# First two batches in three runs over the hidden columns, with the weight conversions spread over 36 units

## The chip, the core and the metric

The kernel runs on one core of a Trainium2 chip. The metric is the device time of one execution in microseconds; of two kernels the one with the lower time is better. A core has five engines that run side by side, each with an in-order queue of its own: PE multiplies matrices into PSUM, DVE and POOL do elementwise work, ACT does activations and copies, and SP issues the DMA transfers. POOL cannot read PSUM.

## The reference

For 8 batches of 8 heads, attention runs twice (32 packed queries `p` attend to `k` and `v`, then `q` attends to the packed result), and two feed-forward layers follow:

```
p_packed = softmax(p @ k.T * scale) @ v
x = softmax(q @ p_packed.T * scale) @ p_packed      # 4608 tokens x 512 after the heads are joined
h = x @ w_in                                        # 512 -> 2048
x = (max(h, 0) + alpha * min(h, 0)) @ w_out         # 2048 -> 512
out = (silu(x @ w_gate) * (x @ w_val)) @ w_out2     # 512 -> 1536 -> 512
```

The inputs of attention are 32-bit floats. The weight matrices are 64-bit floats, and the kernel converts them on the chip.

## The kernel before, in words

**Stage 1** makes attention and the first layer, **stage 2** (`gv_step`) the second layer. Stage 1 is a list `order` of 256 units. A unit is one half batch `j` (288 tokens) and one of 16 groups `f` of 128 hidden columns. `h_unit` makes six matmuls with the attention weights `a2` and the product `ppw` of the packed result with `w_in`. ACT then scales the result (`m`, L1003), DVE makes the activation `g` (L1006), ACT rounds it to `hi` (L1014), and POOL subtracts to get `lo` (L1016). Three units later `o_unit` adds twelve matmuls with `w_out` into four PSUM banks `acc`. At the end of a half batch's run over `f` the four banks are emptied: to DRAM as a partial sum `x1p` if columns are still to come, and with the earlier partial sum added (L1047) otherwise. A run that follows cannot start in the banks until they are empty.

**Order of the units.** Batches 0 and 1 (half batches 0 to 3) share their weights: first f = 0..7 for all four, then f = 8..15 for all four, 64 units in all. The other batches follow one by one.

**Conversion of a weight piece.** `w_in` and `w_out` come as 16 pieces each, `i0`..`i15` and `o0`..`o15`, one per f; an entry `1` in a script calls `convert()` for the next piece of `ORDER`. `widen` loads a piece, takes its high words with ACT (L222), and forms the float on DVE (L224, L228, L237, L246, and L254 for three pieces in four); POOL adds the parts (L265, and L252 in place of L254 for eight pieces). A piece of `w_out` costs two more steps on ACT (L283, L284) and one on POOL (L285). The tiles are called `cva` and `cvb`.

**Attention of batches 0 and 1** is done by `quad` for four groups of heads: a and b are batch 0, c and d batch 1. The scripts name its steps: `c.kt0` turns keys with PE and copies them out of PSUM with ACT (L338), `c.s1`, `c.et`, `c.pp`, `c.ppt` make the packed result, `c.s2` and `c.a2` the second softmax (DVE L497 to L534; for d two of its steps are on POOL). `w01` makes `ppw` of batch 0 for f = 4..7 (PE L795, ACT L799, DVE L800).

**What sets the order of the work around the units** is written by hand. `START` runs ahead of unit 0. `EARLY` has a key (unit, 0 or 1): the script runs ahead of or behind `h_unit` of that unit. `BEHIND` puts loads of c and d behind the load of a certain weight piece in SP's queue. `HOLD` delays four of ACT's L222 steps. From unit `CHAIN0` on, PE takes its work in the order in which it is written; ahead of it a scheduler may order PE's work otherwise. Slots from `GROUP0` on are also given to the conversion of stage 2's weights.

Of the kernel before, what the change touches and what calls it, by code (L numbers as in the profile page):

```python
# [17 lines left out]
P = 128  # L18
# [7 lines left out]
LOADS = "b.v a.v 1", "a.q 1 1 b.q"  # L26
START = """
    a.kt0 b.kt0 a.pt a.kt1 b.kt1 b.pt a.s1 a.et a.pp b.s1 a.ppt b.et b.qt0 a.qt0 b.pp b.qt1 a.qt1
    a.s20 b.ppt b.s20 a.a20 b.a20 1 1 1 1 1 w00 1 1
"""  # L30
EARLY = {
    (0, 0): "c.pd d.pd",
    (0, 1): "c.pt 1 b.s21 c.kt0 c.kt1",
    (1, 0): "c.s1",
    (1, 1): "d.kt0 d.pt 1 c.et d.qt0 c.pp",
    (2, 0): "c.qt0",
    (3, 0): "w01 d.qt1 a.s21",
    (3, 1): "c.ppt b.a21",
    (4, 1): "1 d.kt1 d.s1 a.a21 c.qt1",
    (5, 1): "1",  # L40
    (6, 1): "1 d.et",
    (7, 0): "d.pp",
    (7, 1): "1",
    (10, 1): "c.s2 d.ppt d.s2 w10",
    (11, 1): "1",
    (13, 0): "d.a2",
    (15, 0): "c.a2",
    (17, 1): "w11",
    (18, 1): "1 1",
    (20, 1): "1 1",  # L50
    (21, 1): "1",
    (23, 1): "1",
    (24, 1): "1",
    (25, 1): "1 1",
    (26, 1): "1 1",
    (27, 1): "1 w02",
    (28, 1): "w03",
    (33, 1): "1",
    (36, 1): "w12 w13",
    (37, 1): "1 1",  # L60
}

ORDER = """
    i2 o2 i0 i3 i1 o0 o3 o1 i5 i4 i7 i6 o5 o4 o7 o6
    i13 i10 i11 o13 i15 i8 i14 i9 i12 o10 o14 o8 o9 o12 o11 o15
"""

BEHIND = {"c.k": 3, "c.q": 4, "c.v": 5, "d.k": 5, "d.q": 6, "d.v": 9}

BY_POOL = {0, 2, 4, 7, 11, 18, 23, 29}  # L70
HOLD = {15: 5, 16: 7, 17: 15, 19: 16}


STEPS = """
# [8 lines left out]

LEAVE = (6, 7, 38, 39)

CHAIN0 = 36

# [15 lines left out]
def f32(ap):  # L105
    return ap.bitcast(F32)
# [3 lines left out]
def tile_kernel(  # L110
# [23 lines left out]
    nc = tc.nc  # L134
    B, H, S, D = q.shape
# [79 lines left out]
    def widen(src, raw, val, out=None, n_piece=-1):  # L215

        issued.append(nc.sync.dma_start(out=like(raw, src), in_=src))
        words = raw.rearrange("p (n t) -> p n t", t=2)
        low, high = words[:, :, 0], words[:, :, 1]
        held = n_piece in HOLD  # L220
        with tc.issue_after(begun[HOLD[n_piece]].ins) if held else ExitStack():
            nc.scalar.activation(out=f32(val), in_=f32(high), func=AF.Abs)  # L222
        yield "v"
        nc.vector.tensor_scalar(  # L224
            out=f32(val), in0=f32(val), scalar1=E_TOP, scalar2=E_LOW, op0=ALU.min, op1=ALU.max
        )
# [639 lines left out]
    def at(it, late, fn):  # L866

        plan.setdefault((it, late), []).append(fn)

    order = []
    for bs in [(0, 1)] + [(b,) for b in range(2, B)]:
        for fs in (range(NF1 // 2), range(NF1 // 2, NF1)) if len(bs) > 1 else (range(NF1),):
            for j in range(2 * bs[0], 2 * bs[-1] + 2):
                order += [(j, f, f == fs[0], f == fs[-1]) for f in fs]

    NB1 = 2 * NF1
    busy = set()
# [98 lines left out]
    def load_part(j):  # L978
        part[j] = [utile("x", [P, 2, HS], f"x1p{j}_{pr}") for pr in range(2)]
        for pr in range(2):  # L980
            nc.sync.dma_start(out=part[j][pr], in_=x1p[j][:, 2 * pr : 2 * pr + 2, :])
# [37 lines left out]
    def o_unit(it):  # L1019
# [17 lines left out]
        if not stop:  # L1037
            return
        if f != NF1 - 1:
            x1p[j] = dram.tile([P, KC, HS], F32, name=f"x1p{j}")  # L1040
        dst = x1d[j] if f == NF1 - 1 else x1p[j]
        for pr in range(2):
            xs = part[j][pr] if j in part else utile("x", [P, 2, HS], f"x1s{it}_{pr}")
# [7 lines left out]
                    nc.scalar.activation(out=xs[:, i, :], in_=a, func=AF.Copy)  # L1051
            nc.sync.dma_start(out=dst[:, 2 * pr : 2 * pr + 2, :], in_=xs)

    for j in range(4):
        at(NB1 + 8 * j + 6, 0, lambda j=j: load_part(j))


    raw2, xs2, gvw, wo2, ps2, acc2, outs = {}, {}, {}, {}, {}, {}, {}
# [303 lines left out]
```

## Time and profile before

| what | us |
|---|---|
| time of three executions, median | 1705.68 |
| lowest, highest of them | 1702.39, 1712.24 |
| span of the profiled execution, first to last instruction | 1709.4 |

The profiled execution's time outside its span is not on its page, so the span stands for it: it is 3.7 us over the median and inside the three times. The page divides the span into busy time of engines, and the trace behind it gives every instruction with its start, its duration and what it waited for. Times in the rows are microseconds from the span's start unless marked ns. A busy time counts the time that an instruction takes on its engine, waits inside it included.

### The profile page before, as it was taken

Reading aid. Unit: us, or ns where it says so; the run is one execution under the profiler, and the core shown is the slowest. Engines: PE = TensorE matmul, PEld = TensorE weight load, DVE = VectorE, ACT = ScalarE, POOL = GpSimd, SP = SyncE. Lnnn points to the kernel's source line nnn. Section 1 sums busy time; section 2 is a strip of 40 time slices with the busy share of each in tenths; the row PEclk is TensorE's granted clock in tenths of the full one; section 3 lists DMA queues with packets and bytes.
Section 4 is the critical chain, followed back from the end, with each engine's and each line's share of the span. In section 5 each row is a group of like instructions: output and inputs, shape, how many; then the busy total and the mean of one; then the engine's idle time right before and its main releaser. Section 6 shows DMA issues by size and latency. Waiting matters only on the chain.

```text
span 1709.4 us, 28545 instructions
## 1 busy us (share of the span) xinstructions
PE 1614.0 (94%) x10708; PEld 1458.3 (85%) x10708; DVE 923.8 (54%) x1621; ACT 683.4 (40%) x1511; POOL 804.6 (47%) x824
## 2 busy tenths in 40 slices
PE   5698999999998989999999999999999999999997
PEld 3467798988888878889899999999999999999997
DVE  5989757555656646565533543553453454354332
ACT  5774645545544545555522231232232232123222
POOL 3656744655554654547633443443443443343343
PEclk8899999999999999999999999999999999999999
DMA  9433464635445452644573463455455456445442
GB/s 232 123 103 111 121 161 115 163 95 149 133 117 133 119 139 63 150 128 151 181 275 141 174 235 140 164 198 185 165 209 178 162 184 201 163 173 176 163 173 80
DMA packets 227370, 266.11 MB, mean 156 GB/s; under 512 B 130464, under 2 KB 189856, under 8 KB 227232
## 3 DMA queue, kind: packets, MB, share of 16 engines
q1 hardware_dynamic: 227232, 264.30, 48.8%
q8 instruction: 84, 1.38, 0.3%
q14 instruction: 54, 0.44, 0.1%
HBM read 214.70 MB, written 49.55 MB: 155 GB/s over the span
## 4 chain that ended last, share of the span: by engine, by line
PE 70%; DVE 8%; DMA 6%; POOL 5%; issue 5%; ACT 4%; SPq 2%; DVEq 0%; POOLq 0%; ACTq 0%
PE o L306 6%; PE o L307 6%; PE o L305 6%; PE acc L1029 5%; PE yb L305 4%; PE acc L1035 4%; PE acc L1030 4%; PE yb L307 4%; PE yb L306 4%; PE vb L306 3%; PE vb L307 3%; PE vb L305 3%; PE xb L306 3%; PE xb L307 3%; PE xb L305 3%
## 5 line engine op out<-in xcount | busy, mean ns | idle before, releaser
L1016 POOL TENSOR_TENSOR lo<-g,hi 128x288 fp32r<-128x288 f32 x256 | 226.2, 885 | 244.0 <-ACT hi L1014 188.8
L1223 POOL TENSOR_TENSOR s<-s,p 128x384 f32<-128x384 f32 x72 | 73.2, 1016 | 468.7 <-ACT s L1222 468.7
L1006 DVE SCALAR_TENSOR_TENSOR g<-h,sg,m 128x288 f32<-128x288 f32 x256 | 130.4, 510 | 163.5 <-ACT m L1003 129.0
L305 PE MATMUL h<-a2h,ppw 128*128 128x288 f32 x512 | 163.0, 318 | 27.5 <-DVE g L1006 21.5
L1184 DVE TENSOR_TENSOR u<-vb,u 128x384 f32<-128x384 f32 x144 | 80.3, 558 | 190.5 <-PE vb L307 189.6
L1014 ACT ACTIVATE hi<-g 128x288 fp32r<-128x288 f32 x256 | 113.0, 442 | 155.2 <-DVE g L1006 151.3
L307 PE MATMUL o<-wp,ph 128*128 128x512 f32 x432 | 171.4, 397 | 0.0
L306 PE MATMUL o<-wp,ph 128*128 128x512 f32 x432 | 170.9, 396 | 0.0
L305 PE MATMUL o<-wp,pl 128*128 128x512 f32 x432 | 168.7, 391 | 1.0 <-POOL pl L1249 1.0
L1249 POOL TENSOR_TENSOR pl<-s,ph 128x384 fp32r<-128x384 f32 x144 | 145.4, 1031 | 32.3 <-ACT ph L1247 32.3
L1222 ACT ACTIVATE s<-p 128x384 f32<-128x384 f32 x72 | 37.9, 526 | 301.8 <-DVE p L1184 301.8
L307 PE MATMUL h<-a2l,ppw 128*128 128x288 f32 x512 | 153.3, 300 | 0.0
L306 PE MATMUL h<-a2h,ppw 128*128 128x288 f32 x512 | 153.1, 299 | 0.0
L305 PEld LDWEIGHTS h<-a2h,ppw 128*128 128x128 f32 x512 | 98.4, 192 | 62.3 <-DVE g L1006 30.7
L305 PE MATMUL yb<-ring,gv 128*128 128x384 f32 x432 | 146.0, 338 | 3.6 <-DVE u L1184 3.4
L306 PE MATMUL yb<-ring,gv 128*128 128x384 f32 x432 | 144.4, 334 | 0.0
L307 PE MATMUL yb<-ring,gv 128*128 128x384 f32 x432 | 144.4, 334 | 0.0
L1003 ACT ACTIVATE m<-h,sal 128x288 f32<-128x288 f32 x256 | 125.6, 492 | 44.0 <-PE h L307 43.0
L1184 DVE TENSOR_TENSOR u<-yb,p 128x384 f32<-128x384 f32 x144 | 79.4, 551 | 116.9 <-PE yb L307 107.0
L1247 ACT ACTIVATE ph<-s 128x384 fp32r<-128x384 f32 x144 | 74.7, 525 | 148.3 <-DVE s L1227 133.3
L1229 POOL TENSOR_TENSOR s<-s,u 128x384 f32<-128x384 f32 x72 | 98.9, 1373 | 5.6
L1210 DVE TENSOR_TENSOR s<-xb,s 128x384 f32<-128x384 f32 x72 | 40.1, 557 | 110.0 <-ACT s L1209 110.0
(234 smaller groups left out, 4409.6 us busy)
## 6 DMA issues: line engine op xcount, KB each, us to landing
gv<-wgvd SPq DMA_DIRECT2D x144, 896.0 KB, 6.2
wgvd<-cva SPq DMA_DIRECT2D x84, 256.0 KB, 2.5
cva<-in_moe_w_out_dram SPq DMA_DIRECT2D x28, 512.0 KB, 3.7
v<-in_v_dram SPq DMA_DIRECT2D x16, 576.0 KB, 5.5
out_dram<-os SPq DMA_DIRECT2D x12, 768.0 KB, 3.8
cva<-in_moe_w_in_dram SPq DMA_DIRECT2D x16, 512.0 KB, 4.1
kr<-in_k_dram SPq DMA_DIRECT2D x96, 72.0 KB, 2.7
qr<-in_q_dram SPq DMA_DIRECT2D x96, 72.0 KB, 2.5
```

The lines of the kernel that those rows point to most:

```text
L305: nc.tensor.matmul(o, wlo, xhi, start=start, stop=False, **kw)
L306: nc.tensor.matmul(o, whi, xhi, start=False, stop=False, **kw)
L307: return nc.tensor.matmul(o, whi, xlo, start=False, stop=stop, **kw)
L1003: begun[it] = nc.scalar.activation(out=m, in_=hp, func=AF.Copy, scale=sal[:, f : f + 1])
L1006: made[it] = nc.vector.scalar_tensor_tensor(out=g32, in0=hp, scalar=sg[:, f : f + 1], in1=m, op0=ALU.mult, op1=ALU.max)
L1014: rounded[n] = nc.scalar.activation(out=hi, in_=x, func=AF.Copy)
L1016: nc.gpsimd.tensor_tensor(out=lo, in0=x, in1=f32(hi), op=ALU.subtract)
L1029: nc.tensor.matmul(acc[dc], lo[:, f % WP, c], ghi, start=start, stop=False)
L1184: return nc.vector.tensor_tensor(out=out, in0=bank, in1=x, op=ALU.add)
L1229: nc.gpsimd.tensor_tensor(out=s2, in0=s2, in1=u3, op=ALU.mult)
L1247: nc.scalar.activation(out=hi, in_=x, func=AF.Copy)
L1249: nc.gpsimd.tensor_tensor(out=lo, in0=x, in1=f32(hi), op=ALU.subtract)
```

## The change

The list `order` now goes through the first two batches in three runs over f: columns 0..3 for the four half batches (units 0 to 15), columns 4..7 (units 16 to 31), and columns 8..15 (units 32 to 63, as before). Each half batch therefore stores two partial sums and loads two, where it stored one and loaded one. `ORDER`, `EARLY`, `START`, `BEHIND`, `HOLD` and `CHAIN0` follow:

```
-    a.s20 b.ppt b.s20 a.a20 b.a20 1 1 1 1 1 w00 1 1
+    a.s20 b.ppt b.s20 a.a20 b.a20 1 1 1 1 1 w00
 EARLY = {
-    (0, 1): "c.pt 1 b.s21 c.kt0 c.kt1",
...
-    (10, 1): "c.s2 d.ppt d.s2 w10",
...
-    (36, 1): "w12 w13",
-    (37, 1): "1 1",
+    (0, 1): "c.pt c.kt0 c.kt1",
...
+    (6, 0): "d.a2",
+    (6, 1): "w10",
     (7, 1): "1",
...
+    (36, 1): "1",
+    (44, 1): "w12",
+    (48, 1): "w13",
...
-BEHIND = {"c.k": 3, "c.q": 4, "c.v": 5, "d.k": 5, "d.q": 6, "d.v": 9}
+BEHIND = {"c.k": 3, "c.q": 4, "c.v": 5, "d.k": 5, "d.q": 6, "d.v": 7}
...
-HOLD = {15: 5, 16: 7, 17: 15, 19: 16}
+FIRST_RUNS = (4, 4, 8)
...
-CHAIN0 = 36
+CHAIN0 = 4
...
-        held = n_piece in HOLD
-        with tc.issue_after(begun[HOLD[n_piece]].ins) if held else ExitStack():
-            nc.scalar.activation(out=f32(val), in_=f32(high), func=AF.Abs)
+        nc.scalar.activation(out=f32(val), in_=f32(high), func=AF.Abs)
...
+    for n in FIRST_RUNS:
+        for j in range(4):
+            if f0:
+                again.append((len(order) + n - 1, j))
+            order += [(j, f, f == f0, f == f0 + n - 1) for f in range(f0, f0 + n)]
+        f0 += n
+    for j in range(4, NHALF):
+        order += [(j, f, f == 0, f == NF1 - 1) for f in range(NF1)]
...
-            x1p[j] = dram.tile([P, KC, HS], F32, name=f"x1p{j}")
+            x1p[j] = dram.tile([P, KC, HS], F32, name=f"x1p{j}_{f}")
...
-    for j in range(4):
-        at(NB1 + 8 * j + 6, 0, lambda j=j: load_part(j))
+    for it, j in again:
+        at(it, 1, lambda j=j: load_part(j))
```

Eight pieces are now converted in `START` (ten before), none in units 0 to 6, and the other 24 from unit 7 to unit 36, mostly one a unit. Up to unit 39 both kernels convert all 32.

DVE's queue between the activations `g32_2` and `g32_3` of units 2 and 3, before (`cva` and `cvb` are tiles of a weight piece):

```order
L1006 SCALAR_TENSOR_TENSOR g32_2_732<-h2_725,sg_98,m_2_733 128x288
L246 TENSOR_SCALAR cva1_102<-cva1_102 128x512
L224 TENSOR_SCALAR cvb0_103<-cvb0_103 128x512
L228 TENSOR_SCALAR cvb0_103<-cvb0_103 128x512
L237 SCALAR_TENSOR_TENSOR cvb0_103<-cva0_101,cvb0_103 128x512
L1006 SCALAR_TENSOR_TENSOR g32_3_778<-h3_771,sg_98,m_3_779 128x288
```

The same place in the change (lines have moved by 11 or 16; `s2t_0`, `a_0` are group a's second softmax, `mx_3`, `sums_3` group d's first):

```order
L528 TENSOR_REDUCE sx_0_373<-s2t_0_372 128x9
L529 TENSOR_SCALAR sx_0_373<-sx_0_373 128x9
L530 RECIPROCAL sx_0_373<-sx_0_373 128x9
L427 TENSOR_REDUCE mx_3_703<-s11_3_700 128x1
L531 TENSOR_TENSOR s2t_0_372<-s2t_0_372,sx_0_373 128x288
L427 TENSOR_REDUCE mx_3_703<-s10_3_697 128x1
L545 STREAM_TRANSPOSE a_0_400<-s2t_0_372 128x288
L430 TENSOR_REDUCE mx_3_703<-mx_3_703 128x1
L431 TENSOR_SCALAR mx_3_703<-mx_3_703 128x1
L443 TENSOR_SCALAR sums_3_709<-sums_3_709 128x1
L451 RECIPROCAL sums_3_709<-sums_3_709 128x1
L1022 SCALAR_TENSOR_TENSOR g32_3_763<-h3_756,sg_98,m_3_764 128x288
```

The conversions are gone from here and attention has moved up. Between the activations of units 0 and 8, DVE's queue held the steps of eight pieces and now holds those of two; between units 8 and 39 it held 14 to 15 and now holds 22. On POOL between `lo` of units 8 and 39, L265 goes from 15 to 21, L285 from 8 to 11 and L252 from 3 to 4. The five or so wide steps of c's and d's second softmax on each of the two engines move the other way, from behind unit 8 to ahead of it. From unit 0 to unit 39 the counts of both kernels are the same but for the partial sums and `ppw`.

DVE's queue around units 22 to 25, before:

```order
L1006 SCALAR_TENSOR_TENSOR g32_23_1612<-h23_1605,sg_98,m_23_1613 128x288
L254 SCALAR_TENSOR_TENSOR cva0_101<-cva0_101 128x512
L224 TENSOR_SCALAR cvb0_103<-cvb0_103 128x512
L228 TENSOR_SCALAR cvb0_103<-cvb0_103 128x512
L237 SCALAR_TENSOR_TENSOR cvb0_103<-cva1_102,cvb0_103 128x512
L1006 SCALAR_TENSOR_TENSOR g32_24_1647<-h24_1640,sg_98,m_24_1648 128x288
```

There in the change (`acc0_16` to `acc3_16` are the banks of the run that began at unit 16, `x1p0` the partial sum of half batch 0):

```order
L1022 SCALAR_TENSOR_TENSOR g32_22_1593<-h22_1586,sg_98,m_22_1594 128x288
L248 SCALAR_TENSOR_TENSOR cva1_102<-cva1_102 128x512
L1063 TENSOR_TENSOR x1p0_0_1495<-acc0_16_1523,x1p0_0_1495 128x288
L1063 TENSOR_TENSOR x1p0_0_1495<-acc1_16_1524,x1p0_0_1495 128x288
L1063 TENSOR_TENSOR x1p0_1_1496<-acc2_16_1525,x1p0_1_1496 128x288
L1063 TENSOR_TENSOR x1p0_1_1496<-acc3_16_1526,x1p0_1_1496 128x288
L257 TENSOR_SCALAR cva1_102<-cva1_102 128x512
L1022 SCALAR_TENSOR_TENSOR g32_23_1640<-h23_1633,sg_98,m_23_1641 128x288
```

Four additions stand between the steps of a piece. This occurs four times, at the ends of the second run's half batches, so 16 additions are new in all.

DVE's queue around units 36 and 37, before (`ppw1_2` and `ppw1_3` come of `w12` and `w13`):

```order
L1006 SCALAR_TENSOR_TENSOR g32_36_2092<-h36_2085,sg_98,m_36_2093 128x288
...
L228 TENSOR_SCALAR cva1_102<-cva1_102 128x512
L237 SCALAR_TENSOR_TENSOR cva1_102<-cva0_101,cva1_102 128x512
L800 TENSOR_TENSOR ppw1_2_2100<-ppw1_21_2106,ppw1_2_2100 128x512
L237 SCALAR_TENSOR_TENSOR cva1_102<-cva0_101,cva1_102 128x512
L246 TENSOR_SCALAR cva0_101<-cva1_102 128x512 x2
L800 TENSOR_TENSOR ppw1_3_2111<-ppw1_30_2112,ppw1_3_2111 128x512
L254 SCALAR_TENSOR_TENSOR cva0_101<-cva0_101 128x512 x2
L800 TENSOR_TENSOR ppw1_3_2111<-ppw1_31_2117,ppw1_3_2111 128x512
L1006 SCALAR_TENSOR_TENSOR g32_37_2161<-h37_2154,sg_98,m_37_2162 128x288
```

There in the change:

```order
L1022 SCALAR_TENSOR_TENSOR g32_36_2163<-h36_2156,sg_98,m_36_2164 128x288
L625 STREAM_TRANSPOSE kT0_2_2229<-kr0_2_2146 128x576
L235 TENSOR_SCALAR cva1_102<-cva1_102 128x512
L257 TENSOR_SCALAR cva0_101<-cva1_102 128x512
L239 TENSOR_SCALAR cva1_102<-cva1_102 128x512
L265 SCALAR_TENSOR_TENSOR cva0_101<-cva0_101 128x512
L248 SCALAR_TENSOR_TENSOR cva1_102<-cva0_101,cva1_102 128x512
L1022 SCALAR_TENSOR_TENSOR g32_37_2221<-h37_2214,sg_98,m_37_2222 128x288
```

`w12` and `w13` have left for units 44 and 48. The last pieces are still being converted here, and the last step of the last piece stands just ahead of unit 39's activation.

## Rows read from the trace of the kernel before

**Rows 1.** Stretches: us, busy us (instructions) of PE, PEld, DVE, ACT, POOL, clock, DMA share, GB/s.

```profile
0.00:59.00 59.00, 34.11 (x166) 20.04 (x167) 41.75 (x91) 33.54 (x72) 23.28 (x40) 0.81 0.84 208
59.00:111.00 52.00, 40.60 (x273) 29.93 (x272) 46.59 (x82) 44.58 (x95) 31.69 (x27) 0.95 0.32 97
111.00:206.00 95.00, 84.22 (x533) 69.00 (x532) 84.66 (x136) 51.27 (x109) 62.86 (x55) 0.95 0.41 120
206.00:216.00 10.00, 10.00 (x77) 9.88 (x75) 3.97 (x7) 5.37 (x11) 7.86 (x8) 1.00 0.53 113
216.00:286.00 70.00, 70.00 (x674) 63.48 (x681) 44.75 (x88) 37.58 (x87) 34.83 (x40) 1.00 0.54 147
286.00:858.00 572.00, 536.20 (x4638) 490.67 (x4623) 338.30 (x602) 290.55 (x681) 314.18 (x357) 0.98 0.48 131
858.00:1709.00 851.00, 838.87 (x4364) 775.31 (x4362) 363.75 (x619) 220.57 (x459) 329.85 (x300) 1.00 0.49 177
```

**Rows 2.** DVE in time order: activations of units 0, 8, 39, 64, and one conversion step.

```profile
61.85 0.51 DVE L1006 SCALAR_TENSOR_TENSOR g<-h,sg,m 128x288 f32<-128x288 f32 x1
...
111.19 0.47 DVE L1006 SCALAR_TENSOR_TENSOR g<-h,sg,m 128x288 f32<-128x288 f32 x1
...
204.50 1.28 DVE L254 SCALAR_TENSOR_TENSOR cva<-cva 128x512 f32<-128x512 uint32 x2
...
215.52 0.47 DVE L1006 SCALAR_TENSOR_TENSOR g<-h,sg,m 128x288 f32<-128x288 f32 x1
...
286.38 0.51 DVE L1006 SCALAR_TENSOR_TENSOR g<-h,sg,m 128x288 f32<-128x288 f32 x1
```

**Rows 3.** DVE, four lines, 61 to 193 us: count, ns min/median/max, first and last start.

```profile
L228 DVE TENSOR_SCALAR cvb<-cvb x13: 411/917/1497, 64.0 to 188.5; 128x512 uint32<-128x512 uint32 x13
...
L237 DVE SCALAR_TENSOR_TENSOR cvb<-cva,cvb x13: 677/693/1676, 66.3 to 189.8; 128x512 uint32<-128x512 uint32 x13
...
L254 DVE SCALAR_TENSOR_TENSOR cva<-cva x18: 676/694/1494, 62.9 to 184.6; 128x512 f32<-128x512 uint32 x18
...
L1006 DVE SCALAR_TENSOR_TENSOR g<-h,sg,m x34: 474/505/519, 61.8 to 192.9; 128x288 f32<-128x288 f32 x34
```

**Rows 4.** POOL, four lines, 61 to 193 us: count, ns min/median/max, first and last start.

```profile
L1016 POOL TENSOR_TENSOR lo<-g,hi x32: 795/972/1384, 65.0 to 190.4; 128x288 fp32r<-128x288 f32 x32
...
L265 POOL TENSOR_TENSOR cvb<-cvb,cva x7: 1289/1325/1729, 59.9 to 186.9; 128x512 f32<-128x512 f32 x7
...
L285 POOL TENSOR_TENSOR wo1l<-cvb,wo1h x3: 1287/1499/1587, 87.7 to 97.5; 128x512 fp32r<-128x512 f32 x3
...
L252 POOL TENSOR_TENSOR cva<-cva x4: 1039/1042/1047, 77.3 to 191.6; 128x512 f32<-128x512 f32 x4
```

**Rows 5.** ACT by line, 59 to 110 us: count, busy us, mean ns, idle before.

```profile
L222 ACT ACTIVATE cvb<-cva 128x512 f32<-128x512 f32 x5 | 3.4, 671 | 0.0
L283 ACT ACTIVATE cvb<-cvb,sg 128x512 f32<-128x512 f32 x4 | 2.8, 712 | 0.0
...
L284 ACT ACTIVATE wo1h<-cvb 128x512 fp32r<-128x512 f32 x3 | 1.9, 621 | 0.0
```

**Rows 6.** DVE and POOL in time order, second softmax of c and d.

```profile
113.94 0.75 DVE L502 TENSOR_TENSOR s2t<-s2t,sx 128x576 f32<-128x576 f32 x1
...
119.43 0.83 DVE L497 STREAM_TRANSPOSE s2t<-s 128x288 f32<-128x288 f32 x2
...
121.13 1.16 POOL L502 TENSOR_TENSOR s2t<-s2t,sx 128x576 f32<-128x576 f32 x1 [2.24 <-DVE sx L501]
...
128.86 3.00 POOL L536 TENSOR_TENSOR a2l<-a,a2h 128x576 fp32r<-128x576 f32 x2 [0.72 <-ACT a2h L535]
```

**Rows 7.** Partial sums: additions (ns min/median/max) and the landing of their transfers.

```profile
L1047 DVE TENSOR_TENSOR x1p<-acc,x1p x16: 416/448/458, 224.5 to 296.3; 128x288 f32<-128x288 f32 x16
...
DMA to landing us min/median/max: 2.1/2.7/5.2
```

**Rows 8.** PE by line, 196 to 198 us.

```profile
L795 PE MATMUL ppw<-wi,ppT 128*64 128x512 f32 x8 | 1.9, 605 | 0.0
```

More of the change, by code (lines that the diff above doesn't have):

```diff
@@ L32 @@
     (0, 0): "c.pd d.pd",
-    (0, 1): "c.pt 1 b.s21 c.kt0 c.kt1",
[L34 to L42, printed above, removed]
-    (7, 1): "1",
-    (10, 1): "c.s2 d.ppt d.s2 w10",
[L45 to L50, printed above, removed]
+    (0, 1): "c.pt c.kt0 c.kt1",
+    (1, 0): "b.s21 c.s1",
+    (1, 1): "a.s21 d.kt0 d.pt d.kt1",
+    (2, 0): "b.a21 c.et",
+    (2, 1): "a.a21 d.s1 c.pp",
+    (3, 0): "c.qt0 d.et",
+    (3, 1): "c.ppt d.pp c.qt1",
+    (4, 0): "d.qt0",
+    (4, 1): "d.ppt c.s2 d.qt1",
+    (5, 0): "d.s2",
+    (5, 1): "c.a2",
+    (6, 0): "d.a2",
+    (6, 1): "w10",
+    (7, 1): "1",
+    (8, 1): "1",
+    (9, 1): "1",
+    (10, 1): "1",
+    (12, 0): "w01",
+    (12, 1): "1",
+    (13, 1): "1",
+    (14, 1): "1",
+    (15, 1): "1",
+    (17, 1): "1",
+    (18, 1): "1 w11",
+    (20, 1): "1",
     (21, 1): "1",
-    (23, 1): "1",
+    (22, 1): "1",
     (24, 1): "1",
[L54 to L57, printed above, removed]
-    (33, 1): "1",
-    (36, 1): "w12 w13",
-    (37, 1): "1 1",
+    (25, 1): "1",
+    (26, 1): "1 w02",
+    (28, 1): "1",
+    (29, 1): "1",
+    (30, 1): "1 w03",
+    (32, 1): "1",
+    (33, 1): "1",
+    (34, 1): "1",
+    (35, 1): "1",
+    (36, 1): "1",
+    (44, 1): "w12",
+    (48, 1): "w13",
 }
@@ L64 @@
     i2 o2 i0 i3 i1 o0 o3 o1 i5 i4 i7 i6 o5 o4 o7 o6
-    i13 i10 i11 o13 i15 i8 i14 i9 i12 o10 o14 o8 o9 o12 o11 o15
+    i8 i9 i10 i11 o8 o9 i12 i13 i14 i15 o10 o11 o12 o13 o14 o15
 """
-BEHIND = {"c.k": 3, "c.q": 4, "c.v": 5, "d.k": 5, "d.q": 6, "d.v": 9}
+BEHIND = {"c.k": 3, "c.q": 4, "c.v": 5, "d.k": 5, "d.q": 6, "d.v": 7}
 BY_POOL = {0, 2, 4, 7, 11, 18, 23, 29}
-HOLD = {15: 5, 16: 7, 17: 15, 19: 16}
+FIRST_RUNS = (4, 4, 8)
 STEPS = """
@@ L868, in at @@
         plan.setdefault((it, late), []).append(fn)
[L872 to L876, printed above, removed]
+    order, again = [], []
+    f0 = 0
+    for n in FIRST_RUNS:
[6 more added lines that the diff above has]
+        order += [(j, f, f == 0, f == NF1 - 1) for f in range(NF1)]
     NB1 = 2 * NF1
```

## The prediction

> **What bounds the kernel now.** I read the stretches first [rows 1]. From 858 us to the end PE is busy for 838.87 of 851 us, and from 286 to 858 us for 536.20 of 572. From 216 to 286 us it has no gap at all. These three stretches run at PE's pace, and the change moves nothing in them but two small steps, so whatever unit 64 gains or loses reaches the end unchanged. Only the time ahead of unit 64 is open.
>
> In that time PE is not the bound. From 59 to 111 us it works for 40.60 of 52 us, and from 111 to 206 us for 84.22 of 95. DVE is busy for 46.59 of 52 and then 84.66 of 95 us, and rests afterwards (3.97 of 10). The activations mark the pace [rows 2]: unit 0 at 61.85 us, unit 8 at 111.19, unit 39 at 215.52, unit 64 at 286.38. The last conversion steps on DVE end at 205.78 (204.50 + 1.28).
>
> The next view shows what fills DVE [rows 3]. L228, always of one shape, takes 411 ns at its fastest, 917 in the middle and 1497 at its slowest. L237 and L254 go from 677 and 676 to 1676 and 1494. L1006 reads PSUM and never leaves 474 to 519 ns. So the steps that work in SBUF alone wait inside their own time, and those that read PSUM do not. The wait, up to 1.1 us, is about one POOL instruction. POOL's instructions stretch as well: L1016 from 795 to 1384 ns, L265 from 1289 to 1729 [rows 4]. I read this as DVE's SBUF steps and POOL's steps taking turns at something they share. The amounts fit. From 59 to 206 us POOL is busy for 94.55 us (31.69 + 62.86). The 23 or so pieces that DVE does in that time (8 ahead of unit 8, 14 to 15 behind it) cost about 2.4 us each at the fastest times, some 56 us. Together that is 150 us in a stretch of 147, with POOL's own waiting still inside the first number. Conversions are thus limited by DVE and POOL as a pair, and the pair has hardly any rest from unit 0 to the last piece.
>
> **The change, part by part.** From unit 0 to unit 39 both kernels do the same conversions and attention. What counts is when the pair does them.
>
> *Units 0 to 8.* Six pieces leave this place. Attention of c and d stays and finishes here. ACT loses seven L222 (0.67 us), four L283 (0.71), four L284 (0.62) and one more conversion step, 10.7 us, and gains seven steps of the second softmax, partial sums and packed result, at most 4 us. Its 44.58 busy us [rows 1, 5] become about 38. With the 7.4 us in which it rests there today, unit 8 would be due near 59.5 + 38 + 7.4 = 105 us (unit 0 comes some 2 us sooner, as fewer steps stand ahead of it). But the chain of d now ends right ahead of unit 8. From the first transposition (119.43) to the end of the subtractions for c and d (131.86) it took 12.4 us [rows 6], and little else is there to fill it. I take 110 us, with 105 and 116 as bounds, against 111.19: -1.2 us. Unit 8 comes at about its old time, with fewer pieces done.
>
> *Units 8 to 39.* Seven DVE pieces more stand here. At the fastest times one is three steps of 0.41 us (I price L224 and L246 by L228, of the same shape and kind), one L237 of 0.677 and, for six of them, one L254 of 0.676: 7 x 1.91 + 6 x 0.676 = 17.4 us [rows 3]. POOL gains six L265 (1.289), three L285 (1.287) and one L252 (1.04), 12.6 us [rows 4]. Leaving for the front are POOL's two wide steps (1.16 each) and the two subtractions (3.00), and two wide steps on DVE of 0.75 [rows 6], 6.8 us. The pair has 23.2 us more to do after unit 8.
>
> *Rest it can fill.* DVE rests 10.3 of the 95 us from 111 to 206 [rows 1]. Some of that is waiting for PE and ACT and will stay. I take 7 us as filled, bounds 0 and 10.3.
>
> *The 16 additions* cost 16 x 0.448 = 7.2 us [rows 7]. They read PSUM like L1006, so POOL can work beside them. I take half, 3.6, bounds 0 and 7.2. Their transfers (2.7 us to landing, 5.2 at most) have four units of time each and cost nothing as long as no weight load in SP's queue is late.
>
> *The last piece and unit 39.* Before, 9.7 us lay between the last conversion step (205.78) and unit 39's activation (215.52), used to catch up on matmuls and for `w12` and `w13`. In the change the last step stands directly ahead of that activation, so 9.2 of these are saved (9.7 less one activation).
>
> *`w12` and `w13`* move into the stretch that PE fills entirely. Eight of their 16 matmuls take 1.9 us [rows 8]: +3.9 us.
>
> *Priced at nothing:* `HOLD` (ACT has rest after unit 8: 51.27 of 95 us), the earlier load of d's values (needed after 90 us either way), and PE's fixed order from unit 4. PE has spare time up to unit 39; without that cover an activation that comes late would hold up the next unit's matmuls.
>
> The sum: -1.2 + 23.2 - 7 + 3.6 - 9.2 + 3.9 = +13.3 us. The profiled execution would go from 1709.4 to about 1722.7, and the median of the runs, 3.7 us lower, from 1705.7 to 1719.
>
> The rule that decides between this sum and a smaller one: by the Trainium skill, SBUF — State Buffer, section SBUF: two separate sides, POOL and certain DVE instructions (a fast mode on two ports, or two SBUF inputs) exclude each other at one pair of ports, and whichever is first holds it for its whole instruction. By that rule the 23.2 us stand whole; the stretched L228 and the unstretched L1006 agree with it. If POOL's part could lie beside DVE's, only DVE's own share would count, which is the first rival.
>
> **The rivals.**
>
> *POOL's part lies beside DVE's, and the rest is filled up.* Then 17.4 us of DVE work come and 6.8 us leave (eight wide steps near 0.75 and two transpositions, 0.83 together [rows 6]): -1.2 + 10.6 - 7 + 7.2 - 9.2 + 3.9 = +4.3, or 1710; with all 10.3 us filled, 1707. No difference could be told. For it: POOL rests for 32 of the 95 us. Against it: the stretched rows.
>
> *Faster: PE was starved by the early pieces.* Before, 16 pieces must be ready for the first eight units; now eight serve 16 units. If unit 8 came at 105 us and the rest went at the later pace of 2.98 us a unit (572 us for 192 units [rows 1]), unit 39 would be due at 105 + 31 x 2.98 = 197 and unit 64 at 197 + 70.9 + 3.9 = 272 against 286.4: 1691. It decides if the pair can carry a unit's share in under 3 us. By the fastest times a share is 0.795 for L1016 and 22/31 of a piece at about 4.5 us on both engines (2.4 on DVE, 2.1 on POOL), 4.0 us in all, so DVE and POOL would have to overlap by a quarter.
>
> *A new wait in SP's queue.* Eight stores and eight loads of partial sums are new or moved, and weight loads stand behind some of them in the same queue. A load waits until the half batch before it has been stored (2.7 us, 5.2 at most [rows 7]). If three weight loads lose 3 us each this way and the pair runs dry, +9 more: 1728.
>
> **How the numbers follow.** The time must move by over 0.5% (8.5 us: below 1697.2 or above 1714.2) to be told from no change. The forecast has a chance of 0.55 with a range of 1709 to 1728; about 0.46 of it lies above 1714.2. The first rival has 0.25, the faster one 0.11, and SP's wait 0.09. So faster 0.11, same 0.34, slower 0.55. With the terms at their bounds the sum goes from +0.2 (105 us for unit 8, all rest filled, additions free) to +30 (116 us, none filled, additions whole). Every bound at once on the far side is unlikely, and the near side joins the first rival. 1701 to 1732 leaves out most of the faster rival and the uppermost corner, about 2 in 10.
>
> **What would show it.** In the profile after: unit 8's activation near 110 us, and in the units ahead of it POOL with far more rest than now (31.69 of 52 us busy). Then DVE about 90% busy without a break until unit 39, with L228 stretched as before and unit 39's activation near 225 us (215.5 if I am wrong about the pair, below 205 if the faster rival holds). From there to unit 64, 71 to 76 us. From unit 64 to the end no difference. The prediction fails if POOL and DVE overlap more than the stretched rows say, if c's and d's chain ends much before 105 us, or if the stretch behind unit 64 does not carry the delay on.

## The result and the profile after

The changed kernel takes 1730.62 us (median of 4 runs, 1727.13 to 1731.86). The kernel before, run beside it, takes 1707.16 us (1702.39 to 1712.24). The ratio is 1.0127, with a 95% interval of 1.0108 to 1.0145: slower by more than can be taken for no change. The profiled execution has a span of 1730.1 us, 20.7 us more than before.

The stretches of the changed kernel, with the columns of [rows 1]:

```profile
59.00:111.00 52.00, 34.94 (x243) 25.01 (x241) 28.66 (x63) 37.09 (x84) 18.34 (x18) 0.89 0.13 38
111.00:206.00 95.00, 77.13 (x457) 66.03 (x458) 83.67 (x129) 46.25 (x94) 59.71 (x51) 0.87 0.49 151
...
59.00:232.40 173.40, 135.56 (x855) 114.30 (x854) 138.58 (x234) 98.93 (x210) 98.52 (x85) 0.88 0.40 120
232.40:308.00 75.60, 75.60 (x709) 65.80 (x707) 47.78 (x93) 41.14 (x94) 39.25 (x44) 1.00 0.58 152
308.00:879.00 571.00, 537.64 (x4637) 491.54 (x4622) 336.61 (x602) 290.37 (x681) 314.71 (x357) 0.98 0.48 132
879.00:1730.00 851.00, 838.57 (x4365) 775.52 (x4363) 360.37 (x619) 221.19 (x459) 331.48 (x300) 1.00 0.49 177
```

The last two rows are those of before within 3.4 us of busy time for every engine [rows 1]: behind unit 64 nothing has changed. Ahead of unit 8 DVE now works 28.66 of 52 us in place of 46.59, and POOL 18.34 in place of 31.69. The work that left this place has to be done later.

DVE of the changed kernel in time order, answering to [rows 2]: the activations of units 0, 8, 39 and 64, and the last conversion step of the first layer (L265 is L254 of before). In brackets stands the idle time ahead and what ended it:

```profile
59.73 0.52 DVE L1022 SCALAR_TENSOR_TENSOR g<-h,sg,m 128x288 f32<-128x288 f32 x1 [0.97 <-ACT m L1019]
...
113.08 0.52 DVE L1022 SCALAR_TENSOR_TENSOR g<-h,sg,m 128x288 f32<-128x288 f32 x1 [4.01 <-ACT m L1019]
...
231.04 0.67 DVE L265 SCALAR_TENSOR_TENSOR cva<-cva 128x512 f32<-128x512 uint32 x1
...
232.41 0.52 DVE L1022 SCALAR_TENSOR_TENSOR g<-h,sg,m 128x288 f32<-128x288 f32 x1
...
308.16 0.51 DVE L1022 SCALAR_TENSOR_TENSOR g<-h,sg,m 128x288 f32<-128x288 f32 x1
```

Unit 8 comes 1.9 us later than before, unit 39 16.9 us later and unit 64 21.8 us later. From unit 8 to unit 39 it is 119.3 us in place of 104.3, and from 39 to 64 75.75 in place of 70.86.

What the engines waited for between 59 us and unit 39 tells more than the busy times. First the chain of waits of the kernel before (engine, line and what it waited for: us in total, times, longest):

```profile
DVE g L1006 <- ACT m L1003: 10.6, 7, 3.8
...
ACT m L1003 <- PE h L307: 2.5, 5, 0.9
```

Then that of the changed kernel:

```profile
DVE g L1022 <- ACT m L1019: 21.1, 13, 4.9
DVE s2t L508 <- PE s L414: 5.8, 2, 4.6
...
ACT m L1019 <- PE h L318: 23.5, 18, 3.7
...
PE h L316 <- ACT a2h L546: 7.3, 2, 5.5
```

Read it from the end: where PE gets to a unit's `h` late, ACT's `m` is late, and the activation stands at the head of DVE's queue and waits. Whatever stands behind it in the queue waits too.

DVE rests 173.40 - 138.58 = 34.8 us up to unit 39. Before it was 156.5 - 134.7 = 21.8 us (this row is shown with the experiment on POOL's additions below). Where the rest lies is shown by the stretches on either side of unit 8's activation, first of the changed kernel, then behind unit 8 of the kernel before:

```profile
59.00:113.60 54.60, 36.69 (x250) 26.77 (x249) 29.18 (x64) 38.14 (x86) 19.14 (x18) 0.88 0.17 48
113.60:232.40 118.80, 98.86 (x607) 87.53 (x606) 109.40 (x171) 60.79 (x125) 79.38 (x67) 0.88 0.51 153
...
111.00:215.50 104.50, 93.72 (x605) 78.50 (x604) 88.13 (x141) 56.64 (x119) 70.72 (x62) 0.95 0.42 119
```

Ahead of unit 8 DVE rests 25.4 us where it rested 5.4 [rows 1]. Behind unit 8 it rests 9.4 us where it rested 16.4, and is busy for 21.3 us more. So all of the added rest lies ahead of unit 8, and behind unit 8 it is the work that has grown. DVE's waits for `m` divide in the same way: 11.3 us ahead of unit 8 (1.9 before) and 9.8 behind it (8.7 before).

Ahead of unit 8 few conversion steps stand in DVE's queue that a wait could hold back. Two of its activations and its first conversion step behind unit 0:

```profile
77.47 0.52 DVE L1022 SCALAR_TENSOR_TENSOR g<-h,sg,m 128x288 f32<-128x288 f32 x1 [2.74 <-ACT m L1019]
82.88 0.52 DVE L1022 SCALAR_TENSOR_TENSOR g<-h,sg,m 128x288 f32<-128x288 f32 x1 [4.90 <-ACT m L1019]
...
96.32 0.65 DVE L235 TENSOR_SCALAR cvb<-cvb 128x512 f32<-128x512 f32 x1
```

### The profile page after: what moved, and what is told of

It is laid out like the page before. It is cut to its first block, busy times and chain, and to the rows that moved or that the text cites. A ratio compares the mean times of both kernels' runs of the same rounds, so it can differ in the third digit from the quotient of the medians.

```text
span 1730.1 us, 28602 instructions
## 1 busy us (share of the span) xinstructions
PE 1623.5 (94%) x10708; PEld 1468.3 (85%) x10708; DVE 924.0 (53%) x1637; ACT 684.2 (40%) x1511; POOL 807.4 (47%) x824
## 4 chain that ended last, share of the span: by engine, by line
PE 70%; DVE 8%; DMA 8%; issue 5%; POOL 4%; ACT 4%; SPq 1%; DVEq 0%; POOLq 0%; ACTq 0%
PE o L317 6%; PE o L318 6%; PE o L316 5%; PE acc L1045 5%; PE acc L1046 4%; PE acc L1051 4%; PE yb L316 4%; PE yb L318 4%; PE yb L317 4%; DMA wgvd<-cva 4%; PE vb L317 3%; PE vb L318 3%; PE vb L316 3%; PE xb L317 3%; PE xb L318 3%
## 5 line engine op out<-in xcount | busy, mean ns | idle before, releaser
L1263 ACT ACTIVATE ph<-s 128x384 fp32r<-128x384 f32 x144 | 75.2, 526 | 146.2 <-DVE s L1243 129.8
L318 PEld LDWEIGHTS h<-a2l,ppw 128*128 128x128 f32 x512 | 98.9, 193 | 3.6 <-POOL a2l L547 3.6
```

The lines of the kernel that those rows point to most:

```text
L318: return nc.tensor.matmul(o, whi, xlo, start=False, stop=stop, **kw)
L1263: nc.scalar.activation(out=hi, in_=x, func=AF.Copy)
```

## The experiments

In each of the three groups the kernel before ran on the same chip: median 1713.6 us for the first four, 1712.2 for the next four, 1713.0 for the last four. A ratio is always to it (for the changed kernel, to the 1707.2 us beside it). The table gives for every complete kernel the start of unit 39's activation and DVE's busy time and rest between 59 us and that activation, from the row of its stretches; 59 us, busy time and rest add up to the start of unit 39. "Conversion steps" in the text are DVE's five steps on `cva` and `cvb` (five a piece, or four), counted in the trace between two activations. Which of them run ahead of unit 8 can change by itself when another line of a kernel is changed.

| kernel | ratio (95%) | unit 39 | DVE busy | DVE rest |
|---|---|---|---|---|
| before | 1 | 215.5 | 134.7 | 21.8 |
| before, additions on DVE | 1.0014 (0.9998 to 1.003) | 216.6 | 138.0 | 19.6 |
| before, `w12`, `w13` later | 1.0030 (1.0019 to 1.0041) | 217.1 | 130.9 | 27.2 |
| batch 0 first, `CHAIN0` 36 | 1.0072 (1.0044 to 1.0099) | 226.4 | 138.8 | 28.6 |
| before, `CHAIN0` 4 | 1.0070 (1.0046 to 1.0095) | 226.6 | 134.2 | 33.4 |
| before, batch 1 at unit 8 | 1.0071 (1.0053 to 1.009) | 229.4 | 132.6 | 37.8 |
| change, `CHAIN0` 36 | 1.0079 (1.0063 to 1.0096) | 230.9 | 141.9 | 30.0 |
| change, 8 pieces early | 1.0109 (1.009 to 1.0128) | 232.4 | 135.1 | 38.3 |
| change | 1.0127 (1.0108 to 1.0145) | 232.4 | 138.6 | 34.8 |
| batch 0 first | 1.0081 (1.006 to 1.0102) | 233.4 | 138.3 | 36.2 |
| change, no second-run additions | 1.0136 (1.0121 to 1.0152) | 233.8 | 135.0 | 39.8 |
| change, additions on DVE | 1.0113 (1.0091 to 1.0134) | 234.4 | 140.8 | 34.6 |

### The first theory: pieces left for later

The first theory was that of the prediction: the pair has rest ahead of unit 8, since the pieces were taken from there, and must do their work later. Rivals were the 16 additions, PE's fixed order, and DVE's queue alone.

**Eight pieces put back ahead of unit 8**, the three runs kept:

```
-    (0, 1): "c.pt c.kt0 c.kt1",
+    (0, 1): "c.pt 1 c.kt0 c.kt1",
...
-    (6, 1): "w10",
+    (6, 1): "1 w10",
...
-    (32, 1): "1",
...
-    (36, 1): "1",
```

> The changed kernel with the eight pieces i4..i7 and o4..o7 put back into units 0 to 7 and the other 16 into units 8 to 28; the three runs over f stay. Theory (DVE and POOL as a pair rest in units 0 to 7 and the lost work is paid by unit 39): POOL is busy again for over 26 of the 52 us from 59 to 111 us, unit 39 comes near 215 us, and the time is 1700 to 1716, within 8.5 us of before. Rival (the three runs themselves cost, by their additions, stores, loads and emptied banks): two thirds of the delay stay, 1722 or more.

Measured: 1731.58 us, ratio 1.0109. The theory missed, and the rival's time held. The two stretches of this kernel around unit 8's activation (131.19 us), with the columns of [rows 1]:

```profile
59.00:131.70 72.70, 46.36 (x246) 32.58 (x245) 51.64 (x98) 47.52 (x99) 35.72 (x29) 0.69 0.29 83
131.70:232.40 100.70, 92.08 (x617) 84.42 (x616) 83.46 (x137) 52.51 (x111) 64.72 (x58) 0.94 0.53 157
```

DVE did 51.64 us of work ahead of unit 8 in place of 29.18 (59 to 113.6 us in the changed kernel), but unit 8 came 18.1 us later for it. From unit 8 to unit 39 it then took 18.1 us less, so what was gained behind unit 8 had been spent ahead of it. DVE still rested 21.1 us ahead of unit 8. The waits point to attention that is held up by the pieces: PE waits 12.4 us for `a2h` (7.3 in the change) and ACT, which makes it, 8.4 us for DVE's `a` (5.8). That DVE rests in a stretch does not mean that a piece put there is free.

**The second run's 16 additions and 8 loads left out** (its partial sums then overwrite the first run's):

```
-            if f0:
+            if f0 == 8:
                 again.append((len(order) + n - 1, j))
```

> The changed kernel without the second run's 16 additions and the 8 loads that they need: the second run stores its own sums only, by 8 copies on ACT and 8 on DVE, so the first four columns of batches 0 and 1 are left out of the result. Theory (the pair's work is late, additions hide beside POOL): 0 to 4 us faster than the changed kernel, 1726 to 1731. Rival (the additions and their loads in the queues of DVE and SP cost): 10 us or more faster, 1720 or less.

Measured: 1737.22 us, ratio 1.0136, so nothing is gained. The rival missed, and the theory's 1726 to 1731 was missed too, by the other side. The test is a weak one for DVE: the copies that stand in place of the 16 additions leave it with about half of their time (it is busy for 3.6 us less up to unit 39). Eight loads fewer gained nothing.

**PE's free order up to unit 36 given back to the change:**

```
-CHAIN0 = 4
+CHAIN0 = 36
```

> The changed kernel with CHAIN0 at 36 again, so that PE's order up to unit 36 is free. Theory: within 4 us of the changed kernel, 1726 to 1735. Rival (PE's fixed order makes it wait): at least 10 us faster, 1720 or less.

Measured: 1727.94 us, ratio 1.0079, against 1.0109 to 1.0136 of the three others in this group. It helps by some 0.3 to 0.6% and does not bring the time back, so neither expectation held in full. Conversions moved ahead by themselves: DVE worked 49.02 of 52 us from 59 to 111, and 74 conversion steps ran between the activations of units 0 and 8, where the change has 10. Unit 8 came only at 146.2 us, and unit 39 at 230.9 all the same.

Three versions with the three runs thus have 10, 41 and 74 conversion steps ahead of unit 8 (the change, the eight pieces put back, this one, which has PE's free order too), and their unit 39 comes at 232.4, 232.4 and 230.9 us. Where the pieces stand hardly moves it.

**The addition of a piece's two parts moved from POOL to DVE:**

```
-        nc.gpsimd.tensor_tensor(
+        adder = nc.vector if n_piece >= 0 else nc.gpsimd
+        adder.tensor_tensor(
             out=full if out is None else out, in0=full, in1=other, op=ALU.add
```

> The changed kernel with the last step of all 32 first-layer pieces, the addition L265, on DVE (about 0.68 us, as L254) in place of POOL (1.29 us). If DVE and POOL exclude each other, the pair has 24 x 0.6 = 14 us less to do from unit 0 to unit 39: 1714 to 1724. If DVE's queue alone is the bound and POOL lies beside it, DVE has 24 x 0.68 = 16 us more: 1740 or more.

Measured: 1731.67 us, ratio 1.0113, between the two expectations and no clear difference to the change. Why, the same edit to the kernel before shows best.

> The kernel before, with the addition of each piece's two parts (1.29 us on POOL) made on DVE (about 0.69 us) for the 32 pieces of the first layer. In the changed kernel the same step left the time as it was. If DVE and POOL are bound as a pair up to unit 39, as the prediction had it, some 22 additions behind unit 0 give 0.6 us each: unit 39 about 8 to 13 us sooner, ratio 0.992 to 0.995. If DVE alone is the bound, they cost 15 us: ratio 1.008. If neither is and the queues merely follow one another, unit 39 moves by less than 3 us and the ratio is 0.998 to 1.002.

Measured: 1713.8 us, ratio 1.0014. The kernel before, 59 us to unit 39, as one stretch:

```profile
59.00:215.50 156.50, 134.32 (x876) 108.43 (x875) 134.72 (x222) 101.22 (x214) 102.41 (x88) 0.95 0.38 111
```

The same of this run:

```profile
59.00:216.60 157.60, 134.54 (x871) 109.90 (x872) 138.04 (x251) 102.61 (x216) 70.28 (x64) 0.95 0.41 116
```

One of DVE's groups in the kernel before (count | busy us, mean ns), then the same group and two of the additions in this run:

```profile
L228 DVE TENSOR_SCALAR cvb<-cvb 128x512 uint32<-128x512 uint32 x13 | 11.3, 878 | 0.2
...
L228 DVE TENSOR_SCALAR cvb<-cvb 128x512 uint32<-128x512 uint32 x14 | 8.3, 596 | 0.1
...
L266 DVE TENSOR_TENSOR cvb<-cvb,cva 128x512 f32<-128x512 f32 x8 | 7.3, 918 | 0.0
...
L266 DVE TENSOR_TENSOR wi<-cvb,cva 128x512 f32<-128x512 f32 x7 | 4.7, 677 | 0.0
```

With four smaller groups of 2.8, 2.6, 2.0 and 0.7 us, DVE has 25 additions of 20.1 us more, and yet is busy for only 3.3 us more. Its other steps have become some 17 us shorter, and POOL is relieved of 32.1 us. So at least part of the time inside DVE's stretched steps is a wait for POOL: of 32.1 us that POOL gives up, DVE's other steps get back about half. By the Trainium skill, SBUF — State Buffer, section SBUF: two separate sides, a DVE instruction in a mode on two ports or with two inputs in SBUF and a POOL instruction exclude each other at one pair of ports; this run agrees with it. But unit 39 came no sooner (216.6 us), so the pair's total is not what sets it.

### The second theory: batch 1's attention is due at unit 8

In the three runs unit 8 needs batch 1's second softmax; before, unit 16 did. The second theory was that this chain of short steps costs.

**Batch 0 first**: the changed kernel with batch 0 alone in two runs of 4 columns, then batch 1 in one run of 8, due at unit 16 as before.

```
-FIRST_RUNS = (4, 4, 8)
+FIRST_RUNS = ((0, 1), 0, 4), ((0, 1), 4, 4), ((2, 3), 0, 8), (range(4), 8, 8)
...
-    (4, 1): "d.ppt c.s2 d.qt1",
...
+    (10, 1): "c.s2 d.ppt d.s2 w10",
```

> The changed kernel with another list of units: batch 0 alone in two runs of 4 columns (units 0 to 15), then batch 1 in one run of 8 (units 16 to 31), then columns 8 to 15 for all four as in both kernels. So the pieces are still asked for late (8 before unit 0, 6 in units 0 to 7), 8 of the 16 new additions stay, and batch 1's attention is due at unit 16 again and not at unit 8; its scripts stand where they stood before the change. Theory now, after the misses of the runs so far: what costs is that batch 1's attention, a chain of short steps, is due at unit 8, where it stands in the same in-order queues as the pieces and adds to them whichever way they are placed. By it unit 16 comes near 135 us (144.4 in the changed kernel), unit 39 at 208 to 218 us (232.4), and the time is 1695 to 1712, ratio to the kernel before 0.993 to 1.003. Rival: it is the shorter runs and the pieces left for later (16 to 18 behind unit 8) that cost; then unit 39 comes near 225 to 230 and the ratio is 1.007 to 1.012.

Measured: 1725.36 us, ratio 1.0081, unit 39 at 233.4 us. The theory missed, the rival's ratio held.

**The kernel before with batch 1 due at unit 8**, pieces where they were:

```
+    (4, 1): "1 d.ppt c.s2 d.qt1",
+    (5, 0): "d.s2",
+    (5, 1): "1 c.a2",
+    (6, 0): "d.a2",
...
-    (10, 1): "c.s2 d.ppt d.s2 w10",
...
-            for j in range(2 * bs[0], 2 * bs[-1] + 2):
+            for j in (0, 2, 1, 3) if len(bs) > 1 and fs[0] == 0 else range(2 * bs[0], 2 * bs[-1] + 2):
```

> The kernel before, with one thing of the change: batch 1's attention is due at unit 8. In the first run of 8 columns the half batches go in the order 0, 2, 1, 3 instead of 0, 1, 2, 3, and c's and d's steps and the products w10 and w11 are pulled forward for it as in the change; pieces, runs over f, HOLD and CHAIN0 stay. Theory (the date at which batch 1's attention is due costs): unit 8 at 125 to 133 us, as where eight pieces were put back into the changed kernel (131.2), unit 39 at 226 to 233, time 1719 to 1731, ratio 1.007 to 1.013. Rival (pieces left for later cost): here none are left for later, so unit 39 stays at 213 to 219 and the ratio is 0.998 to 1.003.

Measured: 1725.41 us, ratio 1.0071, unit 39 at 229.4 us, unit 8 at 135.8: about what the theory said. PE waits 7.2 us for `a2h` there and 7.3 in the change, and not at all in the kernel before. Behind unit 8, DVE's waits for `m` are as before (9.4 us, 8.7 before), so this loss arises ahead of unit 8. The early date alone is enough to lose 0.7%, but the run before showed that it is not needed for a loss.

**`w12` and `w13` alone moved to units 44 and 48** in the kernel before:

```
-    (36, 1): "w12 w13",
...
+    (44, 1): "w12",
+    (48, 1): "w13",
```

> The kernel before, with one thing of the change: w12 and w13 moved from behind unit 36 to behind units 44 and 48. Taken alone the prediction has it as +3.9 us behind unit 39 and as part of 9.2 us ahead of it. Theory: between units 36 and 37 (11.8 us before) about 4 us go, units 39 to 64 take 74 to 76 us in place of 70.9, and the time stays within 3 us, ratio 0.998 to 1.002. Rival: the wait between units 36 and 37 is that of the two products on DVE and ACT and not of PE; then most of the 9 us go and only 4 come back, ratio 0.996 to 0.998.

Measured: 1717.41 us, ratio 1.0030 (1.0019 to 1.0041). Neither held in full: units 39 to 64 take 76.0 us (+5.1), as said, and unit 39 comes 1.6 us later, not sooner. Moved alone, the two products cost 5 us and give nothing back.

### What the difference hangs on

**Five of DVE's steps left out of 24 pieces, in both kernels.** The load, ACT's first step and POOL's addition stay. For four of the 24 pieces (those whose fifth step is on POOL) it is four of DVE's steps, one of ACT's and one of POOL's.

```
+        if n_piece < 8:
+            yield "v"
+            nc.vector.tensor_scalar(
+                out=f32(val), in0=f32(val), scalar1=E_TOP, scalar2=E_LOW, op0=ALU.min, op1=ALU.max
...
-        other = f32(low) if out is None else like(f32(low), out)
+        summand = f32(low) if n_piece < 8 else f32(val)
+        other = summand if out is None else like(summand, out)
```

The changed kernel:

> The changed kernel with five of DVE's steps left out for 24 of the 32 pieces (index 8 to 31, all those from unit 7 on): of these, the load, ACT's steps and POOL's addition stay, and POOL adds the part to itself; so the weights of 24 pieces are left out in all but form. If the conversions on DVE and POOL behind unit 8 are the bound, as the prediction had it, units 8 to 39 now go at PE's pace, 2.7 us a unit in place of 3.85 (85 us in place of 119), with unit 8 at 111 to 113 as before: unit 39 near 198, and 30 to 35 us less in all (1695 to 1700 on this chip). If the late attention of batch 1 and PE's own order hold the units up, unit 39 stays above 215. To be compared with the same edit to the kernel before (next run): the attention due at unit 8 leaves a difference of 10 to 18 us at unit 39 between the two; if only the pieces' place makes the difference, under 5 us is left.

The kernel before:

> The kernel before with the same five DVE steps left out for the same 24 pieces (two of them ahead of unit 0, six in units 0 to 7, 16 behind), so that their weights are left out here too. If DVE with its conversions sets units 0 to 8, unit 8 comes 15 to 25 us sooner than 111 us, and unit 39 near 180 to 190; by PE's pace (2.7 us a unit) 85 us lie between the two. If the difference between the two kernels is one of where the conversions stand, this one and the changed one end within 5 us of each other; if it is the attention that is due at unit 8, this one stays 10 to 18 us faster.

Measured: 1696.1 us, ratio 0.9903 (0.9873 to 0.9933), for the changed kernel; 1694.4 us, ratio 0.9889 (0.9861 to 0.9917), for the one before. The two can't be told apart. The stretches of the changed kernel without these steps:

```profile
59.00:111.00 52.00, 39.22 (x263) 29.29 (x262) 22.39 (x54) 38.45 (x87) 19.89 (x20) 0.93 0.25 64
111.00:200.00 89.00, 86.47 (x626) 79.13 (x626) 33.41 (x66) 59.84 (x126) 61.41 (x65) 1.00 0.68 209
```

Those of the kernel before without them:

```profile
59.00:111.00 52.00, 44.10 (x302) 33.42 (x301) 19.88 (x48) 45.48 (x101) 28.06 (x29) 0.94 0.40 122
111.00:200.00 89.00, 87.54 (x605) 74.57 (x605) 33.71 (x61) 54.20 (x114) 52.12 (x55) 1.00 0.45 124
```

DVE works some 40% of the time and PE, from 111 us on, nearly all of it. Unit 39 comes at 193.6 us in the changed kernel and at 196.8 in the other. The changed kernel's unit 39 and time went about as expected. Unit 8 of the other came at 104.6 us, 6.6 us sooner than with the steps and not 15 to 25, and its unit 39 later than the 180 to 190 us expected. In the changed one DVE's activations now wait 54.8 us for `m` up to 200 us, and nothing is lost by it. So neither batch 1's date nor PE's order nor the additions cost much by themselves. They cost where DVE has the conversions of the first layer in the same queue. The recorded sign for the pieces' place (under 5 us between the two kernels) came true, but a kernel without the steps can't tell their place from what else holds them up.

The run also tells where in the change the conversions matter. Without the ten steps that stand ahead of unit 8, that unit comes 5.6 us sooner (107.5 us). From unit 8 to unit 39 it then takes 86.2 us in place of 119.3.

**PE's fixed order alone**, in the kernel before:

```
-CHAIN0 = 36
+CHAIN0 = 4
```

> The kernel before with one thing of the change: CHAIN0 = 4, so PE takes its work in written order from unit 4 on and not only from unit 36 on. The prediction priced it at nothing. In the changed kernel ACT waits 23.5 us for PE's matmuls of h up to unit 39, in the kernel before 2.5 us, which speaks for a price. Theory (the fixed order costs, as an o unit that waits holds up the h behind it): unit 39 at 222 to 232 us and ratio 1.004 to 1.010. Rival (no price): unit 39 at 213 to 218 and ratio 0.998 to 1.002.

Measured: 1725.94 us, ratio 1.0070, unit 39 at 226.6 us: the theory held. Its stretch up to unit 39:

```profile
59.00:226.60 167.60, 137.59 (x866) 111.07 (x866) 134.19 (x222) 101.58 (x213) 101.53 (x88) 0.90 0.37 103
```

And its chain of waits there:

```profile
DVE g L1006 <- ACT m L1003: 25.2, 16, 5.6
...
ACT m L1003 <- PE h L307: 14.7, 15, 2.4
```

DVE is busy as long as before (134.19 us to 134.72) and rests 11.6 us more, and its waits for `m` are 14.6 us more. Here most of these waits lie behind unit 8 (19.5 us, 8.7 before), where conversions stand in the queue. The script of the pieces is that of before, but the order that came out on DVE is not: 36 conversion steps ran ahead of unit 8 in place of 42, and 72 in place of 60 between units 16 and 39. So the run shows what the line costs, and not PE's order apart from what it moved on DVE.

**Batch 0 first, with PE's free order:**

> The kernel with batch 0 in two runs of 4 columns and batch 1 due at unit 16, with CHAIN0 = 36 as before the change in place of 4. There unit 39 came at 233.4 us although batch 1 was due at unit 16 again. If PE's fixed order held it up, unit 39 now comes at 212 to 220 us and the ratio to the kernel before is 0.998 to 1.003. If the later pieces did (16 or more behind unit 8 where before had 14 to 15, and six in units 0 to 7), it stays at 226 to 234 and the ratio above 1.005.

Measured: 1726.09 us, ratio 1.0072, unit 39 at 226.4 us. The free order brings unit 39 forward by 7 us, not the 13 to 21 expected, and nothing in the time can be told from the run with the fixed order. The later pieces' rival held by its numbers but not by its reason: 54 conversion steps ran ahead of unit 8 here, more than the 42 of the kernel before.

### The theory that is left

Up to unit 39 every complete kernel has 131 to 142 us of DVE work, and the table's rest goes from 20 to 40 us. Where DVE rests about 20 to 27 us, unit 39 comes at 215 to 217; where it rests 28 to 40, at 226 to 234. Since work and rest add up to unit 39 and the work varies less, this names no cause. It says that a late unit 39 is more a matter of waits than of work.

Shown by the experiments is this. The difference needs the conversion steps on DVE: without them it is gone. Where the pieces stand hardly matters (10, 41 or 74 steps ahead of unit 8), and neither does POOL's part of them. Batch 1's early date and the line that fixes PE's order each cost 0.7% in the kernel before, and `w12` and `w13` 0.3%. With PE's order fixed, the waits show the way: PE's `h` comes late for an activation that is already at the head of DVE's queue, with conversions behind it.

Not shown is that the change loses its time in that way. Its added rest lies ahead of unit 8, where few conversions stand; behind unit 8 DVE is busy for 109.40 of 118.80 us. What the rows of the change show is that DVE waits ahead of unit 8 for late `m` and for batch 1's attention, and that the work left for later then takes its own time. When pieces are put ahead of unit 8, the units there come later by as much as is gained behind them. Not shown either is how the loss divides: the three parts add up to 1.7% taken alone, and the change costs 1.3%, so they overlap. With PE's order free again, 0.8% is left.

PE's granted clock is lower too, a mean of 0.88 of 2.4 GHz up to unit 39 (0.95 before), where PE is busy for 135.56 of 173.40 us (134.32 of 156.50 before). The kernel with `w12` and `w13` later and the one with PE's order fixed both had 0.90 there, and their unit 39 comes at 217.1 and 226.6 us. So the clock does not make the difference between those two; what share it has in the change stays open. No version came out faster than the kernel before.

## Why the prediction was right, and where its sizes were off

- **Verdict and range.** Slower by over 0.5% had the most weight, and 1730.6 us is inside 1701 to 1732, near its upper end. The forecast of +13.3 us met 20.7 in the span. The account of where the time would lie came true: rest ahead of unit 8, DVE 92% busy behind it, the delay carried to the end. The reason given for it did not (next points), so the range was met in part by luck.
- **Unit 8.** 110 us was taken, 113.08 measured, inside the bounds; 3.1 us of the shortfall. The chain of d is what the prediction named: it took 18.0 us here, from its first transposition (93.82) to the end of its subtraction (111.79), against 12.4 for c and d before, and PE waited 5.5 us for its `a2h`. In between stood the ten conversion steps on DVE (96.32 to 109.07). The 5.8 us that DVE waited for PE's logits `s` belong to c.
- **Units 8 to 39.** The terms 23.2 - 7 + 3.6 - 9.2 give +10.6; measured +15.0. Two errors offset each other in part. The work was priced at 26.8 us (23.2 + 3.6): from 113.6 to 232.4 us DVE is busy for 109.40 us, against 88.13 from 111 to 215.5 before, so 21.3 came. The rest fell from 16.4 to 9.4 us, by 7.0, where the prediction had 16.2 (7 filled and 9.2 ahead of unit 39). That is the step that failed in size: nearly all rest up to unit 39 was taken as fillable. The 9.2 us were not all rest either, since DVE had worked 3.97 us between 206 and 216 us [rows 1].
- **"What counts is when the pair does them."** This step failed as a cause. The steps are on DVE and do set the difference, as the two kernels without them show. But with 10, 41 and 74 of them ahead of unit 8, unit 39 comes within 1.5 us, and taking 32.1 us from POOL moved it by 1.1 us the wrong way. Neither the place of the work nor the pair's total sets unit 39.
- **PE's fixed order was priced at nothing**, with PE's spare time as the cover. The line alone costs 0.7%. PE's spare time was no cover: in that run ACT waits 14.7 us for PE's `h` (2.5 before), and DVE's activations wait with it. As a part of the change, giving the order back is worth 0.3 to 0.6%.
- **The 16 additions**: 3.6 us taken. They took 442 to 449 ns each, and with half of that time gone nothing was gained.
- **`w12` and `w13`**: 3.9 us taken, 4.9 measured in the change and 5.1 alone.
- **Behind unit 64**: from there to the end it took 1423.0 us before and 1421.9 now, so the delay is carried through.
- **L228 "stretched as before"** came true in the sum of the steps, not in the figure that the prediction read. Its 917 ns is the median of one of L228's two groups, that on `cvb` [rows 3]. The same group in the changed kernel is the first line here, the other group the second (count, ns min/median/max, first and last start):

```profile
L239 DVE TENSOR_SCALAR cvb<-cvb x14: 410/418/1397, 98.2 to 216.0; 128x512 uint32<-128x512 uint32 x14
L239 DVE TENSOR_SCALAR cva<-cva x10: 411/672/1407, 114.1 to 226.3; 128x512 uint32<-128x512 uint32 x10
...
L228 DVE TENSOR_SCALAR cva<-cva x10: 409/428/1403, 71.8 to 201.1; 128x512 uint32<-128x512 uint32 x10
```

The third line is the other group before. One median fell and the other rose; such a step is either hardly stretched or two to three times as long, and a median jumps between the two. Over all five steps of a piece the mean is 794 ns before (114 steps up to unit 39) and 806 ns in the change (116).
- **A sum.** With the terms at their near bounds the prediction's sum is +1.4 us (-6.2 + 23.2 - 10.3 - 9.2 + 3.9) and not +0.2. Nothing hangs on it.
- **The rivals.** POOL's part beside DVE's: its 1707 to 1710 us did not come, and relieving POOL moved nothing. PE starved by early pieces: PE does go at 2.8 us a unit (86 us from unit 8 to 39), but only where DVE's steps are left out. SP's queue: its 1728 us is the nearest figure of the three, but leaving out 8 loads gained nothing, and none of DVE's waits in the change up to unit 39 is for a piece's load or for ACT's first step on it (4.4 us before).

## What to carry to other kernels

Rest on the engine that is the bound is worth something only if work put there does not delay the chain that ends the rest. Here DVE rested 25.4 us ahead of unit 8, and eight pieces put there brought unit 8 18.1 us later and unit 39 no sooner. So ask of such a rest what ends it, and what the new work will do to that.

In an in-order queue a step that waits for another engine holds back the steps behind it (25.2 us of such waits for `m` in the kernel before with `CHAIN0` 4, 10.6 without). So look at how long such a step waits at the head and at what stands behind it, and not only at busy shares. An order fixed on one engine (PE here) has to be priced by what it delays on the engine that is the bound, even if the fixed engine itself has time to spare. And after an edit that seems to touch one engine, count the order on the others: here one line moved conversions on DVE.

## What the runs showed of the hardware that was not expected

25 additions of 0.64 to 1.35 us were put on DVE in the kernel before, 20.1 us in all, and its busy time rose by 3.3 us only, since its steps that ran beside POOL's became shorter: L228 went from 878 to 596 ns on average. A busy time on DVE thus holds waiting for POOL inside it, and here the 20.1 us that were moved to DVE added only a sixth of that to its busy time. The exchange did not show in the time of the kernel (ratio 1.0014, 0.9998 to 1.003).
